# A hand-written order of 1433 steps, replaced by another order of the same steps

## The chip, the cores and the metric

One core of a Trainium2 chip runs the whole program. The metric is the device time of one execution in microseconds (us); the median of three executions of the kernel before is 490.09 us. A change of about 1% (4.9 us) is what a measurement of this kernel can tell from no change.

## What is computed

A recurrent layer over 4 batches, 8 heads, 768 positions and 48 channels a head, followed by a low-rank mix over positions and a feed-forward layer on 4 x 768 rows of 384 channels, all float32:

```python
for t in range(S):
    cur = np.einsum('bhd,bhe->bhde', u[None] * kt, vt)
    y[:, :, t] = np.einsum('bhd,bhde->bhe', rt, state + cur)
    state = wt[:, :, :, None] * state + np.einsum('bhd,bhe->bhde', kt, vt)
...
h = xt @ U @ V
u = x + h.transpose(0, 2, 1)
ch = np.maximum(u @ w_ch1, 0.0) @ w_ch2
return (u + ch).astype(np.float32)
```

## The kernel before

The recurrence is cut into 24 chunks of 128 positions, six to a batch. A chunk loads its decays w (`LW`), its r and k by channel (`LRK`), its v (`LV`) and, from the second batch on, r and k by position (`LKR`). VectorE (DVE) makes two scans of the decays (`F`, line 367, and `Q`, line 380) and scales r and k by them (`RP`, line 387, and `KS`, line 392; each may run on GpSimd instead). TensorE (PE) turns k (`KT`, line 482) and multiplies the scores (`AM`, line 495). The scores are merged with a diagonal (`SEL`, lines 430 and 432) by a predicated copy on DVE (`CP`, line 498); then PE multiplies them with v (`YA`, lines 555 and 565), adds the carried state's part (`YZ`, lines 578 and 582) and makes the state's growth (`DS`, line 505), which DVE adds up (`ZA`, line 526). The result is copied out (`XE`) and turned (`XT`, line 616). In the first batch the diagonal comes by a product (`PR`, line 448) and eight PE instructions of two columns (`MD`, line 454); later it comes by DVE or GpSimd (`RK`, `RU`, `RED`, lines 413 to 420).

When six chunks of a batch are done, the mix over positions follows (`GA`, `SELM`, `GSL`, then `HP`, line 690) and makes two blocks u of 384 positions (`UADD`, `UH`, `UL`). A block's feed-forward layer has 12 up steps (`UP`, line 738) and 12 down steps (`DN`, line 774). Each is nine matmuls of 384 columns, because each product is taken as high times high, high times low and low times high. After an up step, ScalarE (ACT) or DVE makes the rectified high part (`HH`, lines 745 and 747) and DVE the low part (`HL`, line 751); a down step needs both parts of three up steps.

The weights come as 26 pieces (12 of w1, 12 of w2, 2 of V, with U a smaller one) in a 64-bit form. Each piece takes a load (`LRAW`, line 249), two ACT instructions (`AB`, `E`), three on DVE (`C1`, `C2`, `C3`, lines 283, 290 and 297), one on GpSimd (`ADD`, line 304), a rounding (`HI`) and a subtraction (`SUB`, line 321). Up step f of a block needs piece f of w1.

Each of these is a step of its own, 1433 in all. Each engine's instructions stand in the order in which the steps are recorded, and each engine runs its own in that order. A string, `ORDER` (line 51), gives it: three digits a step, the first two the step's number, the third says in its lowest bit whether the step runs on its second engine, and in the rest how many filling matmuls stand ahead of it. `plan` (line 127) reads it; nothing else sets the order. A filling matmul (`warm` and `lead`, lines 178 and 182) multiplies constants into the bank that the step is about to overwrite; its only effect is that PE works. Loads are all issued by SyncE (SP), one after another; a load whose buffer isn't free yet holds up all loads behind it. The buffers that matter here are two for w, four for r and k (`LRK`), two for v, seven for raw weight pieces (shared with u), and three PSUM banks for the feed-forward layer.

```python
i, how = DIGITS.index(ORDER[n]) * 64 + DIGITS.index(ORDER[n + 1]), DIGITS.index(ORDER[n + 2])
if how % 2:
    s.eng = s.alt
s.lead = how // 2
```

Of the kernel before, what the change touches and what calls it, by code (L numbers as in the profile page):

```python
# [48 lines left out]

DIGITS = "0123456789ABCDEFGHIJKLMNOPQRSTUVWXYZabcdefghijklmnopqrstuvwxyz+-"  # L50
ORDER = (
    "3n03p01g01F04C00001X03s03r04E03y03u03o03v04D01h01i04e01j01G01k01H05301I01l04L04d04F00200103t13q01Z01J04H01m0"
# [4 lines left out]
    "05x05e06105J05X05f18Y05b05Y05M05g15005K06005h15Z05OA5105i01518O05a05P05w00Q05j05z00B05k00S08p05Q00C00T05R05+"
    "05m08X05l00D08o05S06300E00h00U01b06E06408y05-"
    "06515p01c05N08x06705y08Z18Q05n01d06615q00F00q01e06809F05r00V00i05s80j06901f15t01600W00k05o00H08q00l00s06A00J"
    "00m06B00K09h08a16C60L06D08b00n06F01809O00M00o02W06G08c06H60Y00N10p16I00O10r06J08d01706KE9P06O06S06L02Y06T09Q"  # L60
    "06M06P00a06N16Q01900t06U06R16V16WI1A00u06X01B00v06Y01C00w01D01y01E10x02x00X10Z00y12X06Zm0b02Z00c02a01+00d01z"
    "02b06a12z00e06b02c00f02E00g12d01p01-02y06cc2e12002+02106f02-"
    "02F06d12202G06e01r02H02N06i03002302I06g08z12J06l08+16j12406h02P06k03106o01q08-"
    "06m09R02K09q03206n02509016r0AG01s03312o02L01t08R06p06u06s02O01u09116t01v06q06x02708T02M13D01w08U06v02606y06w"
    "09E02q08V02802Q02903F02R02A06z02B09N02S02f02C01x12D12p06++8r03E02r07108s13G06-"
    "02s02h03H07002T08t07407212U01O03I02V17507303J02g02i03K03402t07602j08u01Q07702k09g08v08W13603L18g07802l01P079"
    "08e09p08h02u03e0A702m03M02v01R08k82n18f02w13507A01S08l03709S11T03808w13f08m03907B03g03h08n09H08i03O03i09J09T"
    "09208j19G03A09409301U03V07C03B09503C01V01W09903N03P07D09M13W03X03Q09I09K07M09A03R0A607N07Q09L19B0AZ09607E07O"
    "09C07R09i03S09W09707S07F09D07T17G0AF09X07P17U09809b07V03Y07W09c09j09U09d03Z09k1D409V09l07X17Y09m09e07Z09Y03a"
    "0AY09f07b07a09n1A809Z03b07e07c09a0Ah03c17d03d17f09o13T19wCA909y09x03j09+0AB03U07g08609-"  # L70
    "03k0AA03l07H0AE1A019r1Ab0AM07h09s1AN0Ag1Ac19t03m0AQ07i1Ai07I09u07j0AH1AC07k08S0AD0D30Ad0AI07J07l07m09v0AJ07n"
    "09z0DD0AK0DC0Aj1AL1AO0Ae07o0A10AP0DT0Af1A20Aa07p0DE0Ao0DU0AR07K0AS1DF07q07L0Dc0Ak1D608707r0Al0DG0Am1Dd07s07t"
    "0E30DW0A30A40DB17u07w0A50DX0D707v0An0D80Db0Ap0Av07x0De0AT07y0D90AU0D50880AV0Dw0E41Dv0DY0DA1AW07z0Df0AX0DH0Dg"
    "0Aq0E51EV07+1DI0E20Ar07-"
    "0DV0Dy0DJ0Dh1EM0800E60As0Dz0E11Ex0DK0DL0EW1810DZ0At0Eo0DN0820Di0Au0EL0D+0DM0830Da1DO1EX1D-"
    "0Aw0840DP0Ax0850En0E00Ay0EU0Dx0EO0890Az0A+0E70EP1EY0ET0Ew0A-"
    "0EQ08C08A0FN0B008B0E80B10ER08D0Eq0FD0C10B308E0FO1Er1B40B20Es0C208F0FP0FM0Ev1B70FG08I0B80B518J0Ey1B61ES0C50B9"
    "1Dj0Et08K0Dk0C31Hk0BA18L0FI0Ez0C608G0Eu1E+08H0C90Hu0BB08M0C40CA0Ht08N0Hn0BE0BC0FJ0Ho1E90BH0BF1Hv0DQ0I80Hp0EA"
    "0BD0BG0Hw0BK0BI1C71BJ0C80IH0DR0BL1BN0CB1DS0BM0CC1FH0BQ0BO1BP0BT0BR1BS0BW0BU1BV0BZ0BX0BY0Bc0Ba1Bb0Bf0Bd1Be0Bi"
    "0Bg0Bh0Bl0Bj0Bk0Bm0Bn0Bo0Br0Bp0Bq0Bs0Bt0Dn0Dl0Do0Dp0ED0Dm0Eb0Bu0Ec0Bx0Bv0Bw0By0Dq0Dr0EZ0EN0EB0Ds0EE0FE0Ea0EF"  # L80
    "0Dt0EC0Bz0Du0FQ0II0B+0FK0FL0Ef0B-0EG0Hq0C00EH0Ep0IJ1F10Ia0EI0Eg0E-"
    "0Hl0CD0F20IK0F01Eh0EJ0IB0CG0EK0Ij0Hx0ID0IC0CJ0Ik0CE1CH0CF0Hr1CI0F50CK0Hs0Ed0CL0IE0H+0Cn0H-"
    "0Ee0Il0J00Id0CM0Im1CP0Ie0If0CN1J90CO0Ei0CQ0CR0Ej0FR1FF0F30F60I90Ek0CS0F71F40FS1F80CT0IL0IG0FT0CU0Hy1Hm0JA0F9"
    "0IF0Hz1J30Co0Ib0FA0Ig0El0In0I20JS0Em0J50CV0J40Jc0JB1I30FU0JC0CY0CW0Ih0Jb0CX0FB0J60CZ0Cb0FC0Ii1Ju0Ca0Jd0FV0Cc"
    "0Cd0Je0FW0IA0Cp0FX0J10IM0K10JV0FY0IN0Ce0JX0FZ0JW0JD0K20Ch0J70Cf1J81IO0Cg0I00IP0Ci1JY0IS0JT0Fa0K31Cj0Iq0IT0Ck"
    "0Ir0I10IU1K41JG0Cl1I40JH0Ja1IQ0Cm0Io0Ic0JZ0Ip1Cq0IR0Jf0Ct0Jx0Cr0Cu0Jz0Jy0Cs0J+0Cv0Cw0Cz0Cx0Cy0C+0C-"
    "0D00Is0D10D20Iu0It0Fb0Ji0Fc0JI0Jj0I50Fd0IV0Fe0Ff0IW0JE0J20Gi0IX0Iv0Jv0Gm0Gq0JF1Gj0I60Ix0Gr0Gn0I70Fg0JJ0Iw1JU"
    "0IY0Fk0Fo0Iy0Jg1K50Fl0K00JK0Fp0IZ0Jk0JL0Iz0Jh0Fh0JN0J-0Fi0Jl0Fj0JO0K61Jw0I+0Fm1K80JM0I-"
    "0Fn1Fq0K70Jm0Gk0Fr0Fs0K90Go1Gl1Fv0Gs1Gp1Gt1Jn0Fy0Fw0Ft1Jo1Fx0Fu0F-"
    "0Fz1F+0GQ0G01G10G20G50G31G40G80G60G70GR0G91GA0GB0GE0GC0GD0GH0GF0GG0GK0GI0GJ0GN0GL0GM0GS0GO0GP0GT0GW0GU0GV0GX"  # L90
    "0GY0GZ0Gc0Ga0Gb0Gd0Ge0Gf0Gu0Gg0Gh0Gx0Gv1Gw0G+0Gy0JP0Gz0H10G-"
    "0H00JQ0H21H40JR0H30H70H50H60HA0H80H90HS0HB1HC0HT0Jp0Jq0HD0Jr0HG0HE1HF0HJ0HH0HI0HM0HK0HL0HP0HN0HO0HU0HQ1HR0Js"
    "0KA0Jt0KB0KF0KC0HV0KD0HW0HY0KE0HX0KG0HZ0KH0KI0Ha0KJ0KK0KL0KP0Hb0KM0KQ0KN1KR1KT0KO0He0Hc0KU0Hd0KS1KV0LN0KW1LR"
    "0Hf0LO0LS0LP0LT0LQ0Hg0LU1Hh0LV0KX0Hi0LW0Hj0LX1LY1Ka0KY0KZ0Kd0Kb1Kc0Kg0Ke0Kf0L50Kh0Ki0Kj0Km0Kk1Kl0Kp0Kn1Ko0L6"
    "0Kq0Kr0Ks0Kv0Kt1Ku0Ky0Kw0Kx0L70Kz0K+0K-"
    "0L20L00L10L30L40L80LB0L90LA0LC0LD0LE0LH0LF0LG0LI0LJ0LZ0LK0La1Lb0Lc0LL0LM0Lf0Ld0Le0Li0Lg0Lh0M70Lj0Lk0Ll0Lo0Lm"
    "1Ln0Lr0Lp1Lq0M80Ls0Lt0Lu0Lx0Lv1Lw0L+0Ly1Lz0M90L-"
    "0M00M10M40M21M30M51M60MA0MD0MB0MC0ME0MF0MG0MJ0MH0MI0MK0ML0MM0MN0MO0"
)


# [885 lines left out]
```

## Time and profile before

| what | us |
|---|---|
| median of 3 executions (488.08 to 491.03) | 490.09 |
| the profiled execution | 493.23 |
| its span, first to last instruction | 491.4 |
| PE busy | 467.2 |
| DVE busy | 315.2 |
| ACT busy | 169.5 |
| GpSimd (POOL) busy | 114.6 |

The profile is of one execution. PEld is the loading of weights into the array; it overlaps PE. The clock of PE is granted at one of two levels, 2.4 GHz (1.0 in the rows) and 1.2 GHz (0.5). Filling matmuls count as busy.

### The profile page before, as it was taken

To read this page: it belongs to the slowest core of one execution; us is meant where nothing else is said; L and a number is where in the kernel's file an instruction comes from. 1 tells how busy PE (TensorE), PEld (TensorE's weight loads), DVE (VectorE), ACT (ScalarE), POOL (GpSimd) and SP (SyncE) were. 2 spreads that over 40 slices of the span, in tenths; PEclk is the share of its full clock that TensorE was granted. 3 is DMA by queue.
4 is the path that set the end of the run, shared out by engine and by line. 5 is a ranking of instruction groups with operands and counts; after the bars stand their busy time and mean duration, and the time that the engine had idled before them with its cause. 6 is when DMAs were issued, how large, how long until landed. Compare 5 with 4: busy or idle time off the path is not lost.

```text
span 491.4 us, 9913 instructions
## 1 busy us (share of the span) xinstructions
PE 467.2 (95%) x4116; PEld 419.8 (85%) x4116; DVE 315.2 (64%) x543; ACT 169.5 (34%) x430; POOL 114.6 (23%) x106
## 2 busy tenths in 40 slices
...
PEclk9656999999999999999999999999999999999998
...
GB/s 295 258 70 173 232 234 128 176 130 147 148 85 88 168 269 111 108 1 16 79 166 120 192 99 33 99 21 0 17 32 1 1 34 17 1 27 23 0 18 37
DMA packets 20644, 47.38 MB, mean 96 GB/s; under 512 B 2480, under 2 KB 8880, under 8 KB 20592
## 3 DMA queue, kind: packets, MB, share of 16 engines
...
q8 instruction: 34, 0.56, 0.5%
q14 instruction: 18, 0.15, 0.1%
...
## 4 chain that ended last, share of the span: by engine, by line
PE 57%; DVE 21%; DMA 10%; ACT 4%; issue 4%; POOL 2%; SPq 0%; POOLq 0%; DVEq 0%; ACTq 0%
PE f L774 23%; PE f L738 22%; DMA raw_w<-in_w 4%; DMA w<-in_wT 3%; DVE Q L380 3%; DVE F L367 3%; DMA rk<-in_rkT 3%; PE aps L495 2%; DVE cva_w L297 2%; DVE hl L751 2%; PE y L555 1%; PE trk L482 1%; PE y L565 1%; DVE rk L392 1%; PE dS L505 1%
## 5 line engine op out<-in xcount | busy, mean ns | idle before, releaser
L738 PE MATMUL f<-u,w1h 128*128 128x384 f32 x576 | 158.1, 344 | 2.0 <-DVE hl L751 1.4
L738 PEld LDWEIGHTS f<-u,w1h 128*128 128x128 f32 x576 | 105.4, 188 | 4.8 <-DVE hl L751 2.5
L774 PE MATMUL f<-hh,w2h 128*128 128x384 f32 x288 | 100.0, 347 | 0.0
L738 PE MATMUL f<-u,w1l 128*128 128x384 f32 x288 | 97.6, 339 | 0.0
L774 PE MATMUL f<-hh,w2l 128*128 128x384 f32 x288 | 97.5, 339 | 0.0
L751 DVE SCALAR_TENSOR_TENSOR hl<-f,hh 128x384 fp32r<-128x384 f32 x96 | 52.5, 552 | 34.6 <-ACT hh L745 33.4
L745 ACT ACTIVATE hh<-f 128x384 fp32r<-128x384 f32 x56 | 27.3, 488 | 128.0 <-PE f L738 128.0
L774 PE MATMUL f<-hl,w2h 128*128 128x384 f32 x288 | 66.3, 338 | 0.0
L774 PEld LDWEIGHTS f<-hh,w2h 128*128 128x128 f32 x288 | 54.0, 188 | 3.5 <-issue 1.7
L774 PEld LDWEIGHTS f<-hh,w2l 128*128 128x128 f32 x288 | 54.1, 188 | 0.3
L738 PEld LDWEIGHTS f<-u,w1l 128*128 128x128 f32 x288 | 54.1, 188 | 0.2 <-DVE w1l L321 0.2
L774 PEld LDWEIGHTS f<-hl,w2h 128*128 128x128 f32 x288 | 52.0, 188 | 0.0
L789 DVE TENSOR_TENSOR xT<-f,xT 128x384 f32<-128x384 f32 x24 | 13.3, 553 | 55.6 <-PE f L774 55.5
L747 DVE TENSOR_SCALAR hh<-f 128x384 fp32r<-128x384 f32 x40 | 22.2, 554 | 32.2 <-PE f L738 32.0
L304 POOL TENSOR_TENSOR cva_w<-cva_w,raw_w 128x384 int32<-128x384 int32 x24 | 29.8, 1247 | 40.8 <-DVE cva_w L297 21.7
L432 POOL TENSOR_SCALAR_AFFINE_SELECT A<-dv 128x512 f32<-128x512 f32 x23 | 19.5, 855 | 84.4 <-PE y L565 46.4
L498 DVE COPY_PREDICATED A<-maskf,aps 128x1024 f32<-128x1024 uint32 x24 | 31.4, 1307 | 7.1 <-PE aps L495 4.6
L367 DVE TENSOR_TENSOR_SCAN F<-w,resets 128x517 f32<-128x517 f32 x24 | 32.5, 1354 | 2.5 <-DMA w<-in_wT 1.4
L430 ACT ACTIVATE A<-ident,dv 128x128 f32<-128x128 f32 x100 | 31.6, 390 | 5.1 <-DVE dv L461 2.3
L495 PE MATMUL aps<-rk 48*128 48x128 f32 x384 | 30.6, 303 | 2.2 <-DVE rk L392 1.3
L495 PEld LDWEIGHTS aps<-rk 48*128 48x128 f32 x384 | 25.7, 204 | 6.1 <-issue 2.6
L380 DVE TENSOR_TENSOR_SCAN Q<-w,qd 128x516 f32<-128x516 f32 x24 | 30.5, 1273 | 0.0
...
## 6 DMA issues: line engine op xcount, KB each, us to landing
...
```

The costliest lines, as they stand in the source:

```text
L304: lambda: nc.gpsimd.tensor_tensor(out=d["to"].bitcast(I32), in0=d["a"].bitcast(I32), in1=d["e"], op=ALU.add),
L367: nc.vector.tensor_tensor_scan(out=F[:, ::-1], data0=st["w"][:, ::-1], data1=resets[:, ::-1], initial=1.0, op0=ALU.mult, op1=ALU.add)
L380: nc.vector.tensor_tensor_scan(out=st["Q"], data0=st["w"][:, 0:n], data1=qd, initial=0.0, op0=ALU.mult, op1=ALU.add)
L430: nc.scalar.activation(A[:, i, j], ident, AF.Copy, scale=dv[:, NP * i + j : NP * i + j + 1])
L432: nc.gpsimd.affine_select(out=A[:, i], in_=dv[:, NP * i : NP * i + NP].unsqueeze(2).broadcast_to([P, NP, P]), pattern=[[0, NP], [1, P]], c ...
L495: nc.tensor.matmul(aps[:, i, j, :], rk[r, 1, j, :], rk[r, 0, j, :], start=True, stop=True)
L498: nc.vector.copy_predicated(flat(st["A"]), mask8, flat(st["aps"]))
L738: nc.tensor.matmul(ps, wt[:, f, ct, :], u[ct][:, z], start=(n == 0), stop=(n == 8))
L745: nc.scalar.activation(hh, d["ps", f], AF.Relu)
L747: nc.vector.tensor_scalar(out=hh, in0=d["ps", f], scalar1=0.0, scalar2=None, op0=ALU.max)
L751: nc.vector.scalar_tensor_tensor(out=hl, in0=d["ps", f], scalar=0.0, in1=hh.bitcast(F32), op0=ALU.max, op1=ALU.subtract)
L774: nc.tensor.matmul(d["o", ct], wt[:, 4 * ct + part, f - 3 * part, :], hid[f][z], start=(part == 0 and n == 0), stop=(part == 3 and n == 8),)
```

## The change

Only the string is replaced. The set of steps, their functions, buffers and dependences are the same. The diff is 47 lines of digits on either side, of which one each:

```diff
-    "3n03p01g01F04C00001X03s03r04E03y03u03o03v04D01h01i04e01j01G01k01H05301I01l04L04d04F00200103t13q01Z01J04H01m0"
+    "3n01g01F03p00004C01X03s03r04E03y03u03o03t03v01h01i04D01j01G04d01k00104e01I00201l01H05304F04L03q01Z01J04H01m0"
...
```

Read out, the new string differs in three ways: the order, the second engine for some steps (DVE has 518 steps instead of 529, ACT 300 instead of 296, GpSimd 106 instead of 99), and the filling matmuls (71 instead of 146; 31 ahead of the first `MD` in both). Before, the other 115 stand mostly ahead of the first block's up steps: 9, 24, 19 and 31 ahead of its steps 0, 1, 2 and 10. Now the other 40 stand ahead of `KT` of chunk 0 (6), `YA` of chunk 5 (22), `XT` of chunk 5 (4), `SELM` of batch 0 (4), `AM` of chunk 6 (2) and `YA` of chunk 6 (2), and none in the feed-forward layer.

The first place is SP's queue, between the loads of the first chunks. The names end in a buffer number; raw_w_3 and raw_w_0 ahead of the larger numbers are pieces 3 and 0 of w1, w the decays of a chunk. Before, pieces 3, 4 and 6 of w1 stand here:

```order
L340 DMA w_642<-in_wT 128x517
L352 DMA v_657<-in_vN 128x448
L344 DMA rk_675<-in_rkT 128x1024
L340 DMA w_698<-in_wT 128x517
L249 DMA raw_w_3_708<-in_w 128x768
L348 DMA kr_719<-in_rkN 128x768
L352 DMA v_758<-in_vN 128x448
L249 DMA raw_w_4_780<-in_w 128x768
L344 DMA rk_784<-in_rkT 128x1024
L249 DMA raw_w_6_819<-in_w 128x768
```

In the new order they stand here:

```order
L344 DMA rk_304<-in_rkT 128x1024
L249 DMA raw_w_0_362<-in_w 128x768
L249 DMA raw_w_3_373<-in_w 128x768
L340 DMA w_397<-in_wT 128x517
L352 DMA v_413<-in_vN 128x448
L340 DMA w_429<-in_wT 128x517
L249 DMA raw_w_4_502<-in_w 128x768
L249 DMA raw_w_6_526<-in_w 128x768
L340 DMA w_529<-in_wT 128x517
```

Before, w_642 and w_698 are the decays of chunks 6 and 7, and the three pieces are queued around and behind them; now w_397, w_429 and w_529 are those of chunks 4, 5 and 6, and the pieces stand ahead of them.

The second place is DVE around the predicated copy of chunk 0 (`A` written under `maskf`, L498). F and Q are scans, rk and kr the scaled and multiplied r and k, cva a weight piece in work. Before:

```order
L387 TENSOR_TENSOR rk_153<-rk_153,Q_155 128x512
L448 TENSOR_TENSOR kr_258<-rk_162 128x512
L392 TENSOR_TENSOR rk_157<-rk_157,F_176 128x512
L283 TENSOR_SCALAR cva_w_8_197<-cva_w_8_197 128x384
L461 COPY dv_272<-trd_251 128x8
L498 COPY_PREDICATED A_246<-maskf,aps_260 128x1024
L380 SCALAR_TENSOR_TENSOR Q_298<-w_139,qd 128x516
```

Now:

```order
L290 TENSOR_SCALAR cva_w_5_273<-cva_w_5_273 128x384
L297 SCALAR_TENSOR_TENSOR cva_w_8_195<-raw_w_8_143,cva_w_8_195 128x384
L297 SCALAR_TENSOR_TENSOR cva_w_5_273<-raw_w_5_189,cva_w_5_273 128x384
L367 SCALAR_TENSOR_TENSOR F_320<-w_166,resets 128x517
L448 TENSOR_TENSOR kr_323<-rk_171 128x512
L367 SCALAR_TENSOR_TENSOR F_328<-w_248,resets 128x517
L392 TENSOR_TENSOR rk_171<-rk_171,F_320 128x512
L283 TENSOR_SCALAR cva_V_292<-cva_V_292 96x384
L403 RECIPROCAL qd<-F_320 128x4
L498 COPY_PREDICATED A_254<-maskf,aps_276 128x1024
L526 TENSOR_TENSOR Z_364<-dS,Z_315 128x384
```

The copy that PE waits for in chunk 0 has moved back behind the scans of chunks 2 and 3 and the work on weight pieces 8 and 5.

The third place is PE at the start of the feed-forward layer: hp is the mix, f an up step, aps, trk, y, trx and dS the products of a chunk. Before (the pair of a weight load and a filling matmul into f_0_0_0 comes nine times):

```order
L690 MATMUL hp_0_0_893<-Vst,gs_884 128x384
L690 MATMUL hp_0_1_903<-Vst,gs_884 128x384
L690 MATMUL hp_0_2_905<-Vst,gs_884 128x384
L180 LDWEIGHTS resets
L180 MATMUL f_0_0_0_924<-resets 128x384
L180 LDWEIGHTS resets
L180 MATMUL f_0_0_0_924<-resets 128x384
```

Now:

```order
L690 MATMUL hp_0_2_990<-Vst,gs_958 128x384
L482 MATMUL trk_992<-ident,rk_660 128x128 x4
L180 LDWEIGHTS resets
L180 MATMUL y_1002<-resets 128x384
L180 LDWEIGHTS resets
L180 MATMUL y_1002<-resets 128x384
L555 MATMUL y_1002<-A_912,v_797 32x128 x8
L565 MATMUL y_1002<-A_912,v_797 32x128 x8
L616 MATMUL trx_0_1051<-ident,xT_0_1038 128x128 x3
L505 MATMUL dS<-v_797,kn_1044 48x48 x8
L738 MATMUL f_0_0_0_1069<-u_0_0_1032,w1h 128x384
L738 MATMUL f_0_0_0_1069<-u_0_0_1032,w1l 128x384
```

Chunk 6, the first of the second batch, now stands ahead of and within the first block's up steps, where filling matmuls stood.

## Rows read from the trace of the kernel before

**Rows 1.** The page's second part: PE's granted clock in 40 slices of the span.
```profile
PEclk9656999999999999999999999999999999999998
```
**Rows 2.** Busy time by stretches: sum and count of PE, PEld, DVE, ACT, POOL; clock; DMA.
```profile
12.00:24.00 12.00, 8.08 (x72) 6.50 (x72) 11.97 (x14) 7.97 (x23) 6.88 (x6) 0.71 0.83 269
24.00:36.00 12.00, 11.25 (x136) 9.52 (x135) 7.72 (x13) 8.39 (x27) 2.36 (x2) 0.50 0.19 62
36.00:48.00 12.00, 11.37 (x139) 9.68 (x131) 7.75 (x11) 7.48 (x22) 4.51 (x4) 0.66 0.52 166
48.00:60.00 12.00, 10.85 (x194) 7.86 (x191) 10.23 (x19) 8.14 (x24) 5.15 (x4) 1.00 0.77 225
...
84.00:96.00 12.00, 11.28 (x64) 10.76 (x63) 11.97 (x27) 8.08 (x22) 5.41 (x5) 1.00 0.51 181
```
**Rows 3.** The chain that ended last: start, us, what; in a stretch at full clock.
```profile
240.54 0.57 PE y L555 x16
242.21 1.09 PE aps L495 x16
...
249.12 0.59 PE trk L482 x4
249.71 1.59 PE f L738 x9
```
**Rows 4.** PE's instructions in order of time: start, us, what, idle before it.
```profile
13.97 1.05 PE L454 MATMUL trd<-u_diag,kr 128*128 128x2 f32 x8 [2.27 <-POOL kr L448]
...
38.02 2.08 PE L495 MATMUL aps<-rk 48*128 48x128 f32 x16
...
72.35 0.48 PE L738 MATMUL f<-u,w1h 128*128 128x384 f32 x1
...
74.90 4.08 PE L180 MATMUL f<-resets 128*128 128x384 bf16 x24
...
97.35 5.21 PE L180 MATMUL f<-resets 128*128 128x384 bf16 x31
102.26 0.47 PE L738 MATMUL f<-u,w1h 128*128 128x384 f32 x1
...
110.49 0.34 PE L774 MATMUL f<-hh,w2h 128*128 128x384 f32 x1
...
201.89 0.41 PE L738 MATMUL f<-u,w1h 128*128 128x384 f32 x1
...
483.46 0.34 PE L774 MATMUL f<-hh,w2h 128*128 128x384 f32 x1
```
**Rows 5.** DVE's instructions in order of time.
```profile
12.82 1.30 DVE L297 SCALAR_TENSOR_TENSOR cva_U<-raw_U,cva_U 128x192 uint32<-128x192 uint32 x1
14.05 1.75 DVE L387 TENSOR_TENSOR rk<-rk,Q 128x512 f32<-128x512 f32 x1
...
21.70 0.68 DVE L387 TENSOR_TENSOR rk<-rk,Q 128x512 f32<-128x512 f32 x1
22.30 1.23 DVE L367 TENSOR_TENSOR_SCAN F<-w,resets 128x517 f32<-128x517 f32 x1
...
24.29 0.55 DVE L297 SCALAR_TENSOR_TENSOR cva_w<-raw_w,cva_w 128x384 uint32<-128x384 uint32 x1
...
29.66 1.28 DVE L498 COPY_PREDICATED A<-maskf,aps 128x1024 f32<-128x1024 uint32 x1
...
36.43 0.56 DVE L526 TENSOR_TENSOR Z<-dS,Z 128x384 f32<-128x384 f32 x1 [2.67 <-PE y L582]
...
40.65 1.29 DVE L498 COPY_PREDICATED A<-maskf,aps 128x1024 f32<-128x1024 uint32 x1 [2.52 <-PE aps L495]
```
**Rows 6.** SP's issues in order of time, around the third weight load.
```profile
53.85 0.33 SPq L340 DMA_DIRECT2D w<-in_wT  x1
54.23 1.48 SPq L249 DMA_DIRECT2D raw_w<-in_w  x1
```
**Rows 7.** POOL's instructions in order of time.
```profile
15.22 1.62 POOL L392 TENSOR_TENSOR rk<-rk,F 128x512 f32<-128x512 f32 x1
```

More of the change, by code (lines that the diff above doesn't have):

```diff
@@ L57 @@
[L57 to L98, printed above, removed]
+    "3n01g01F03p00004C01X03s03r04E03y03u03o03t03v01h01i04D01j01G04d01k00104e01I00201l01H05304F04L03q01Z01J04H01m0"
+    "1K01n00z04G00301o10401Y01L03z11M00700503++3w01a04m04I01N15201b03-"
+    "13x04014M042C4100+00604404304J00P00901000804K10-"
@@ new lines @@
+    "04605U01105B04R01c01204714g00R04n14S04h15504N04l15610A04i04V01d04504O04P14s01300G04W01e04j04X10h04804Q11f15T"
+    "04k04T05700I05C14f04905804t00i04A00B01405u00k04B00C00j04o00l05c05W04w04p04q15D00m05X01515d16105Y05914U04r15b"
+    "04u00Q05E05A00n05H04v00D00o00q04Y05I05Z00E01600S08O05i05a05400T00s05x04Z05j05e00U01805v05y14x05F04a05z08X00F"
+    "05J05f14y10V04b05L00r05+00Y04z04c05G14+06218Y08o05V00p10W06304-08P05K06001705g18y01905k05-"
+    "00a01A00t05O05h11B00u00X15P06405w08x00v05005l08p01C05Q05100w06511y05R05M05p05N02x05S08Z15m06618R06E08Q00H05q"
@@ new lines @@
+    "05n08z00x06708T01D09F05r00J08a11+05s08U05t02z05o09E08V00K06801E00Z00L069i8b09N00M09O06A08q08c02N06B00N18d19h"
+    "00b06C80O10c08r06D02y06F00d06G08s02+08+16H82-02P08W16I03008g46J09P08-"
+    "06K08t03108h09019q06O06S08e09Q02E03206T08k4A709116P00e06L09R06M02W08u08l0AG06Q08f06N19g06U08m06R12G08i08v08n"
+    "06V16W00f09G08j10y10g18w12F02O03312Y02H02Q01z02I06Z06X02R02J09p01-"
+    "02S09S12006c06Y02K06a19T12T06b01p06f06d02L12o02102U06e02M06i06g02206h02X01r06l02Z02303D02V16j02412q02a01q06k"
+    "09402p02b02r06o01s09502c03F02d02501t09902s01u06p11v09A06m16r06q09B01O06n01w02e12701x13E09C02t06s06u03G09D06t"
@@ new lines @@
+    "02u02601Q03H06x02f02806v03I02v02906w03J06+06y02A03K03402w17102h06z02B01P06-"
+    "13L12C03e01R09202g02D1720AZ02i07403501S02j09301T03602k09607301U03g07007509i09702l01V03M01W02m03V07602n13f037"
+    "03h07M03807703i03903N07N03O03A07O07A07803X03P03B07907P13Q07B03j03R09H07Q07U07C07R03C09I19817V09J03S07D03W03k"
+    "03T03U07G03l07E07F03m07H07S19M17W07T19U07X17Y03Y09V09K03Z09Y0A607Z09j07b03a09k17a09o09l09Z07e07c19a19L17d09w"
+    "0AF03b09W07f09m09x07h09X0AY09n19+07g07i09y03c17j03d17k0A90Ah0AH17n0AA0AB0AE07l17m0AI08607o07p0Ab07I09r1Ac1Ag"
@@ new lines @@
+    "17J0AC08S0AD0D307q0Ad09s07K07L0Ae0AM07r0870AN07s0DT0DC0Af07t09t0AJ0Ai09u0DD0D607w07u0Dc0DW09b07x07v09v0DX17y"
+    "09c0Aj0A809z08809d0D40AK09-"
+    "0DE0AL1D809e0Ak0AO0A01D90A109f0AP0Dv0DA17z0Aa0Al0DF1Am1Dd0A20DB17+1AQ0A30DU0DG0Ao0E20AR0E307-"
+    "0An1A40AS0AT0DY0De0A50Ap0AU0DH0D50Av0Db0AV0Dw0DJ0Aq0DI0DK0E40Ar0DV0Df1DN0As0EM0Dy0AW0800AX0DO0Dz1E51Dg0E10At"
+    "0810DL0E60EV0Au0820Ex0Dh0Aw0DM0Eo0Di0Dj0Ax0830DZ0Dk0D70Da0EL0Ay0841EW0E90D+0Az0850890EA0Ey0A+0EX0C108C08A0EU"
+    "0Ez0C208B0EY0EO0FN0A-0B308D0B40ET0B00B70B108E0D-"
```

26 lines of the change are left out of this document (22 added, 4 removed).

## The prediction, made before the changed kernel ran

> **What bounds the kernel now.** I read the busy time by stretches first, then PE's instructions in order of time with their idle times, then DVE's. A core with one long matmul queue is bounded by PE, and PE's busy share says nothing here, because filling matmuls count as busy. So I keep a ledger. PE's work ahead of a step is the sum of all real steps ahead of it at their full-clock durations, without fills: 1.59 for each up or down step, 1.09 for the scores, 0.59 for the turning of k, 0.57 and about 0.45 for the two halves of the product with v [rows 3], and for the other steps 0.2 to 1.0, taken in the same way from start to start behind 44 us. The start of a step less this work is the time that PE has lost so far.
>
> Before, the first real step starts at 13.97 with nothing done: 14.0 lost. The first up step starts at 72.35 with 32.9 of work ahead: 39.5 lost. The fourth down step of the first block starts at 110.49 with 56.8 ahead (six MD, five KT, six AM, six YA, twelve up and three down steps and the small ones): 53.7. The first up step of the second batch starts at 201.89 with 141.2 ahead: 60.7. The last down step starts at 483.46 with 420.0 ahead: 63.4 [rows 4]. Behind 202 us PE loses 2.7 in 280 us. All that can be won lies between 14 and 202 us.
>
> What causes that loss changes. From about 17 to 44 us (0.71 over 12 to 24, 0.50, then 0.66 over 36 to 48) the clock is at its lower level, 0.5, and small steps take twice their time (scores 2.08 against 1.09) [rows 1 to 4]; there PE is the engine the others wait for: DVE is busy 7.72 and 7.75 us of 12 and has single waits of 2.67 and 2.52 us on PE [rows 2, 5]. From 48 us on DVE is busy 10.23 to 11.97 of 12 and sets the pace [rows 2]; PE then waits, and the table fills the waits: 24 and 31 fills take 4.08 and 5.21 us [rows 4], 0.158 each from start to start. The up steps start at once behind them, so these rows don't tell whether the fills outlast the waits.
>
> For DVE I keep the same ledger: the durations of its instructions ahead of a step in the table's order, at undisturbed rows (1.23 a scan, 1.28 a predicated copy, 0.68 a scaling, 0.55 the third step of a weight piece, and small ones) [rows 5]. Ahead of the first up step stand 91 DVE instructions, 56.0 us; it started at 72.35, so DVE's lag, time less work, was 16.4. At the fourth down step it was 110.49 - 93.4 = 17.1; at 201.89, with 179.9 of work, 22.0.
>
> **The change, part by part.**
>
> *The fills.* 75 of 146 go. At 0.158 that is 11.9 us of PE time. By itself it is worth between nothing (the fills stood in waits for DVE, and without other work PE waits as long) and 11.9. I take nothing, as DVE is busy almost without a stop there [rows 2], and count the real work that takes their place. That is chunks 6 and 7.
>
> *The real work moved in.* Ahead of the first up step PE now has 36.5 of work instead of 32.9 (one AM, KT, YA, XT and DS more, 3.6). Ahead of the fourth down step it has 65.0 instead of 56.8.
>
> *What DVE must have done.* Ahead of the first up step stand 118 instructions, 72.0 us, instead of 91 and 56.0: two more of either scan (4.9), four more second and third steps of weight pieces (3.6), two scalings, a predicated copy, two reductions, and small ones. At the fourth down step it is 103.3 instead of 93.4. So the feed-forward layer starts later and then runs without stopping. Over the whole kernel DVE's work falls by 4.7 us, as 11 of its steps go to ACT and GpSimd, which have idle time beside it (ACT 8.08 of 12 busy, POOL 5.41) [rows 2].
>
> *DVE's lag, the number that decides.* Ahead of the predicated copy of chunk 2 DVE has 32.7 of work instead of 26.5, that is 6.2 us of weight pieces and scans of later chunks. Before, it sat idle for 8.5 us between 24 and 48 us (24 less 7.72 and 7.75) [rows 2]. The weights for this are there: pieces 3, 4 and 6 of w1 were queued behind the decays of chunk 7, issued at 53.85 [rows 6], and are now queued ahead of the decays of chunks 4 to 6. So I take 5.4 off the lag. Bounds: nothing (the waits only move), and 8.5 (all of the idle time). The middle is near the 6.2 that the order can put there, less a wait for r and k of chunk 5, which are now queued behind the decays of chunk 6.
>
> *The sum.* First up step: 72.0 + 11.0 = 83.0, 10.7 us later than before; PE has lost 83.0 - 36.5 = 46.5, seven more than before at that step. Between there and the fourth down step DVE has 31.3 of work and PE 28.5, so both are nearly full; I let the lag grow by 1.7 instead of the 0.7 of before, to 12.7. The step then starts at 103.3 + 12.7 = 116.0, with 116.0 - 65.0 = 51.0 lost: 2.7 less than before. From there to 202 us PE lost 7.0 before: ten fills (1.6), waits for DVE, and the changes between kinds of steps. The new table has no fills there, and DVE's own limit has room: ahead of the first up step of the second batch it has 177.7, with a lag of 17 that is 194.7, while PE with 144.0 of work comes there at about 199. I take 4.0. At the end PE loses 2.7, as before. Total 51.0 + 4.0 + 2.7 = 57.7 instead of 63.4: 5.7 us won. The profiled execution would go from 493.23 to 487.5; it lies 3.1 above the median, so the median goes from 490.09 to 484.4.
>
> *Fills against the clock.* PE had waits of up to 2.27 us and the clock fell at 17 us [rows 2, 4]; from 48 us to the end, with shorter waits and the fills, it stayed at 1.0 [rows 1, 2]. The Trainium skill's page "TensorE: Matmul & The Clock Gate", section "HAM oscillation — how this bites in real kernels", says that waits between bursts of matmuls put the array back on its lower clock, and so speaks against taking fills out. The trace agrees for 17 us. By that rule the stretch before the first up step, where PE has 7.7 of work and 12 fills in 15 us, could lose the clock; by the rows it keeps it, because 22 fills stand right ahead. I keep it in the sum, and make the fall a rival.
>
> *More on GpSimd.* A scaling on DVE took 1.75 us instead of 0.68 while GpSimd ran one of 1.62 [rows 5, 7]. The skill's page "SBUF — State Buffer", section "SBUF: two separate sides", says that the two share a port pair which one of them holds for a whole instruction; the row agrees. GpSimd has seven steps more: by that rule DVE could lose up to seven times 1.1, 7.7 us, and nothing would be won; by the rows it is less, since most of its steps run beside DVE instructions of undisturbed length.
>
> **The rivals.**
>
> *The lag stays.* DVE waits for the cold PE at other places: the scores of chunks 2 and 4 still stand right ahead of the copies that need them. For it: these waits were on PE [rows 5]. Against it: there is now other DVE work between. Lag 17.6 at the fourth down step: 103.3 + 17.6 - 65.0 = 55.9, plus 6.7 is 62.6: 489.3, no change.
>
> *The array stays cold (the slower side).* The first chunks now go at DVE's pace, so PE may never be dense enough before 48 us to get its clock back. Up to the second half of chunk 1 (13.9 of work, about 43 us) the forecast has it cold anyway. From there to the product with v of chunk 5 there are 14.9 of work; at half clock 29.8, so 72.8, and 22 fills at 0.32 bring it to 79.8, where the forecast has 68. The chain from there to the first up step takes some 13.5 (93), DVE's 31.3 and the growth of 1.7 give 126 for the fourth down step: 61.0 lost, and with 6.7 more 67.7: 494.4. It decides if the clock comes back later than about 60 us. For it: 27 us at 0.5 before. Against it: PE has more to do than it can at half clock, so it will be dense.
>
> *The clock falls between 68 and 83 us.* The first two up steps then take 3.2 each; 3.2 us: 487.6.
>
> *All of the idle time is used.* Lag 9.5 at the fourth down step: 47.8 lost, and 3.0 and 2.7 behind it: 53.5, so 480.2.
>
> **How the numbers follow.** Forecast 0.46, within 481 to 488; the lag stays 0.18; cold 0.15; the clock falls 0.08; all used 0.13. About 1% (4.9 us) is what a measurement can tell from no change. Faster by over 1% (below 485.2): the last case and some seven tenths of the forecast, 0.46. Slower by over 1% (above 495.0): most of the cold case, as its price is a lower one if the fills don't bring the clock back, 0.12. The rest, 0.42, lies within. The range leaves out part of the cold case above and of the last one below: 479.5 to 494.5.
>
> **What would show it.** Right: the first up step near 83 us, ten us later than before; DVE busy over 10 of 12 us from 24 us on; the clock back by 50; no stop of PE over 1 us in the first block; the second batch's first up step near 199. The forecast is wrong if the fourth down step starts behind 119 us, or if PE's loss between there and 200 us is 7 or more.

## The result, and the profile of the changed kernel

The changed kernel takes 482.94 us (median of 4 executions, 482.59 to 484.70); the kernel before, measured again beside it, takes 490.56. The ratio is 0.9862, with a 95% interval of 0.9823 to 0.9902: faster, by 1.0 to 1.8%. The forecast was 484.4. The profiled execution took 483.14 with a span of 481.4, against 493.23 and 491.4 before; so the two traces differ by 10.0 us where the medians differ by 7.6, and the traces' differences are to be read with that in mind.

First the page's busy times and PE's clock, to be held beside [rows 1], then the busy times by stretches, with the columns of [rows 2]:

```profile
PE 449.4 (93%) x4041; PEld 409.8 (85%) x4041; DVE 314.6 (65%) x532; ACT 171.2 (36%) x446; POOL 119.9 (25%) x113
...
PEclk9786999999999999999999999999999999999999
```

```profile
24.00:36.00 12.00, 8.18 (x105) 6.88 (x105) 12.00 (x19) 10.60 (x34) 2.12 (x2) 0.83 0.58 191
36.00:48.00 12.00, 10.11 (x108) 8.44 (x110) 9.75 (x15) 6.45 (x19) 6.07 (x6) 0.60 0.33 96
48.00:60.00 12.00, 9.40 (x217) 7.74 (x215) 11.26 (x20) 12.00 (x39) 5.40 (x5) 1.00 0.87 295
...
72.00:84.00 12.00, 8.54 (x97) 6.45 (x96) 11.91 (x23) 9.12 (x26) 3.79 (x4) 1.00 0.71 250
```

PE's busy time fell by 17.8 us (467.2 to 449.4) while the traced time fell by 10. The real matmuls are the same in both, so what went is fills and time at the lower clock. From 24 to 48 us DVE is busy 21.75 us instead of 15.47. The clock is not one stretch at 0.5 as before, but comes and goes until 45.6 us, and is full from there to 479.

PE's instructions in order of time, with the up and down steps of [rows 4]: the fills and the turning of k of chunk 0, the first up step, the fourth down step, the first up step of the second batch, the last down step:

```profile
18.22 2.08 PE L180 MATMUL trk<-resets 128*128 128x384 bf16 x6 [4.07 <-DVE dv L461]
20.09 1.06 PE L482 MATMUL trk<-ident,rk 128*128 128x128 f32 x4
...
81.77 0.44 PE L738 MATMUL f<-u,w1h 128*128 128x384 f32 x1
...
112.96 0.33 PE L774 MATMUL f<-hh,w2h 128*128 128x384 f32 x1
...
194.50 0.42 PE L738 MATMUL f<-u,w1h 128*128 128x384 f32 x1
...
473.55 0.34 PE L774 MATMUL f<-hh,w2h 128*128 128x384 f32 x1
```

With the real work ahead of each step (36.5, 65.0, 144.0 and 420.0 us in the new order) PE's ledger reads as follows. "Lost" is the start of a step less this work.

| step | lost, before | forecast | lost, after |
|---|---|---|---|
| first up step | 39.5 | 46.5 | 45.3 |
| fourth down step | 53.7 | 51.0 | 48.0 |
| first up step of the second batch | 60.7 | 55.0 | 50.5 |
| last down step | 63.4 | 57.7 | 53.5 |

DVE's lag (start less DVE's work ahead) at the first up step is 81.77 - 72.0 = 9.8, at the fourth down step 112.96 - 103.3 = 9.7; before it was 16.4 and 17.1. The busy times from 12 us to the first up step, before and now, show where the lag went: DVE sat idle for 12.4 us then and for 4.9 now.

```profile
12.00:72.35 60.35, 51.31 (x623) 38.62 (x623) 47.99 (x74) 40.35 (x112) 24.98 (x22) 0.77 0.62 199
```

```profile
12.00:81.77 69.77, 52.18 (x706) 38.80 (x703) 64.84 (x102) 49.15 (x141) 26.94 (x26) 0.85 0.62 206
```

What PE waited for longest, from the view of waits (us in total, times, longest); all three are DVE:

```profile
PE trk L180 <- DVE dv L461: 4.1, 1, 4.1
PE y L555 <- DVE A L498: 3.4, 5, 1.3
PE aps L495 <- DVE A L498: 2.9, 2, 1.9
```

DVE had waits of 2.67 and 2.52 us on PE in [rows 5]. Between 24 and 48 us one is left, ahead of the predicated copy of chunk 2 (the second row; the first is the copy of chunk 1):

```profile
38.16 1.27 DVE L498 COPY_PREDICATED A<-maskf,aps 128x1024 f32<-128x1024 uint32 x1
41.67 1.32 DVE L498 COPY_PREDICATED A<-maskf,aps 128x1024 f32<-128x1024 uint32 x1 [2.25 <-PE aps L495]
```

### The profile page after: what moved, and what is told of

Read it like the earlier page. It is cut to its first block, busy times and chain, and to the rows that moved or that the text cites. A ratio compares the mean times of both kernels' runs of the same rounds, so it can differ in the third digit from the quotient of the medians.

```text
span 481.4 us, 9783 instructions
## 1 busy us (share of the span) xinstructions
PE 449.4 (93%) x4041; PEld 409.8 (85%) x4041; DVE 314.6 (65%) x532; ACT 171.2 (36%) x446; POOL 119.9 (25%) x113
## 4 chain that ended last, share of the span: by engine, by line
PE 70%; DVE 16%; DMA 5%; ACT 4%; issue 3%; POOL 1%; SPq 0%; ACTq 0%; DVEq 0%; POOLq 0%
PE f L774 29%; PE f L738 28%; PE aps L495 3%; DVE F L367 3%; DVE A L498 2%; DMA v<-in_vN 2%; PE y L555 2%; DVE cva_w L297 1%; DMA raw_w<-in_w 1%; PE trk L482 1%; DVE Q L380 1%; PE y L565 1%; PE trx L616 1%; DMA rk<-in_rkT 1%; DVE cva_w L283 1%
## 5 line engine op out<-in xcount | busy, mean ns | idle before, releaser
L738 PE MATMUL f<-u,w1h 128*128 128x384 f32 x576 | 157.0, 343 | 1.6 <-DVE u L705 0.8
L738 PEld LDWEIGHTS f<-u,w1h 128*128 128x128 f32 x576 | 105.3, 188 | 4.5 <-DVE u L705 1.5
L738 PE MATMUL f<-u,w1l 128*128 128x384 f32 x288 | 97.5, 338 | 0.0
L745 ACT ACTIVATE hh<-f 128x384 fp32r<-128x384 f32 x52 | 25.2, 486 | 137.6 <-PE f L738 137.5
L738 PEld LDWEIGHTS f<-u,w1l 128*128 128x128 f32 x288 | 54.1, 188 | 0.0
L747 DVE TENSOR_SCALAR hh<-f 128x384 fp32r<-128x384 f32 x44 | 24.2, 552 | 31.0 <-PE f L738 30.7
L430 ACT ACTIVATE A<-ident,dv 128x128 f32<-128x128 f32 x112 | 35.6, 392 | 24.8 <-PE y L565 16.1
L498 DVE COPY_PREDICATED A<-maskf,aps 128x1024 f32<-128x1024 uint32 x24 | 31.5, 1313 | 11.4 <-PE aps L495 5.7
L304 POOL TENSOR_TENSOR cva_w<-cva_w,raw_w 128x384 int32<-128x384 int32 x24 | 28.3, 1182 | 42.1 <-DVE cva_w L297 16.7
L432 POOL TENSOR_SCALAR_AFFINE_SELECT A<-dv 128x512 f32<-128x512 f32 x20 | 15.9, 804 | 75.5 <-PE y L565 58.9
L380 DVE TENSOR_TENSOR_SCAN Q<-w,qd 128x516 f32<-128x516 f32 x24 | 32.5, 1354 | 0.1
```

The costliest lines, as they stand in the source:

```text
L304: lambda: nc.gpsimd.tensor_tensor(out=d["to"].bitcast(I32), in0=d["a"].bitcast(I32), in1=d["e"], op=ALU.add),
L380: nc.vector.tensor_tensor_scan(out=st["Q"], data0=st["w"][:, 0:n], data1=qd, initial=0.0, op0=ALU.mult, op1=ALU.add)
L430: nc.scalar.activation(A[:, i, j], ident, AF.Copy, scale=dv[:, NP * i + j : NP * i + j + 1])
L432: nc.gpsimd.affine_select(out=A[:, i], in_=dv[:, NP * i : NP * i + NP].unsqueeze(2).broadcast_to([P, NP, P]), pattern=[[0, NP], [1, P]], c ...
L498: nc.vector.copy_predicated(flat(st["A"]), mask8, flat(st["aps"]))
L738: nc.tensor.matmul(ps, wt[:, f, ct, :], u[ct][:, z], start=(n == 0), stop=(n == 8))
```

## The experiments

Twelve kernels ran; all change the string only. Ratios are to the kernel before. In four of them (without fills, and with the old engines throughout) the string has eight lines fewer, so their rows name lines that are eight lower: L738 is L730 there.

### The fills

Before, the order as it was, without 115 of its 146 fills (the third digit of a step holds them; one step of eleven is shown):

```diff
-6Zm   (UP 0.0.1 of batch 0, 24 fills)
+6Z0
```

> The order before, without the 115 fills behind the first 31; nothing else. Mine (VectorE sets the pace behind 48 us, the fills stand in waits for it): 490 +- 3, the waits of TensorE grow by what the fills took. Rival A, the fills outlast the waits: up to 18 us faster (115 x 0.158), 472 to 485. Rival B, the fills hold the clock: the clock goes back to 0.5 somewhere between 60 and 110 us and the time is 494 or more.

Measured: 495.41 us, ratio 1.0103 (1.0056 to 1.0150): slower, and rival B's case. The busy times by stretches:

```profile
72.00:84.00 12.00, 8.55 (x25) 7.14 (x24) 9.84 (x24) 6.41 (x13) 5.07 (x5) 0.50 0.41 131
...
96.00:108.00 12.00, 7.06 (x30) 6.75 (x29) 10.59 (x21) 6.95 (x17) 2.36 (x3) 0.72 0.47 151
```

PE's waits between 70 and 113 us in the same run, and its first up step and fourth down step:

```profile
PE f L730 <- DVE w1l L313: 7.3, 2, 4.9
```

```profile
70.08 0.69 PE L730 MATMUL f<-u,w1h 128*128 128x384 f32 x1 [2.45 <-ACT u L691]
...
112.11 0.34 PE L766 MATMUL f<-hh,w2h 128*128 128x384 f32 x1
```

The first up step comes 2.3 us earlier (70.08), as no fills stand ahead of it: here the fills did outlast the wait. But PE now waits 7.3 us for two weight pieces, with no fills in these waits, and the clock falls to 0.5 for the whole of 72 to 84 us and again in 96 to 108. By the tenth up step (95.44, before 95.65) the lead is used up; in the eleventh PE waits 4.9 us for its piece and then runs at 0.5. The fourth down step comes at 112.11: 55.3 lost, 1.6 more than before. So the fills did hold the clock, and taking them out costs more than it saves: 1.6 us there by the traces, 4.0 by the medians (the kernel before took 491.44 beside this run).

The new order without its other 40 fills, and without only the six ahead of the turning of k of chunk 0:

```diff
-69i   (YA 5, 22 fills, and five more steps: 40 fills)
+690
-42C   (KT 0, 6 fills: the second kernel, this step alone)
+420
```

> The new order, without the 40 fills behind the first 31; nothing else. Mine: 483 +- 3 as VectorE sets the pace. Rival B, the fills hold the clock: it falls to 0.5 in 60 to 85 us, or does not come back at 22 us, and the time is 486 to 494. Rival A: up to 6 us faster (40 x 0.158), 477 to 480.

> The new order without the 6 fills ahead of the turning of k of chunk 0 alone. Rival D, these 6 fills bring the clock back at 21.7 us and that is worth something: the clock stays at 0.5 from 15 to 44 us as before, 485 to 490. Mine: the clock there may well stay low, but TensorE waits for VectorE there, so 483 +- 2.

Without the 40: 485.69 us, ratio 0.9890 (0.9847 to 0.9934). The interval overlaps that of the changed kernel, so the 2.8 us between the medians are not sure by themselves. The time lies in my own range; the clock does what rival B said, and the trace has a like sum there. The busy times and the first up step:

```profile
72.00:84.00 12.00, 9.91 (x67) 5.95 (x67) 10.88 (x21) 7.47 (x20) 4.20 (x4) 0.50 0.66 236
```

```profile
84.62 0.69 PE L730 MATMUL f<-u,w1h 128*128 128x384 f32 x1
```

The clock is 0.5 over 72 to 84 us where it is 1.00 with the fills, and the first up step comes at 84.62 instead of 81.77, 2.9 later. What the lower clock by itself costs is not shown by this, for two reasons. The profiled execution is the slowest of its four (487.23, mean granted clock 0.940); the fastest took 483.65 at 0.966. And the fills don't hold the clock all the way: this kernel's fell at 68.8 us, while in all eight traces that keep the 22 fills and the order of the changed kernel up to the first up step it is 1.00 over 60 to 76 us; but in seven of these eight it then goes to 0.5 for 3.4 to 10.2 us between 76 and 89. The changed kernel's own trace is the one exception, and its other three executions have lower mean clocks (0.971, 0.964 and 0.963 against 0.976). The longest such fall is in the kernel below that relieves GpSimd:

```profile
72.00:84.00 12.00, 7.89 (x82) 6.30 (x79) 10.33 (x20) 9.05 (x25) 1.98 (x2) 0.67 0.61 212
```

There the clock is 0.5 from 76.0 to 86.3 us, and the fourth down step comes at 112.69, no later than the changed kernel's 112.96.

Without the six: 484.40 us, ratio 0.9872 (0.9831 to 0.9913), no difference that can be told. The clock still comes back, at 23.4 us, but for 3.4 us only; over 24 to 36 us it is 0.62 instead of 0.83, and chunk 1's scores start at 30.96 instead of 30.65:

```profile
24.00:36.00 12.00, 8.78 (x86) 7.13 (x86) 12.00 (x19) 8.78 (x27) 2.42 (x2) 0.62 0.48 169
```

DVE is busy 12.00 of 12 in either, so a faster PE gains little there. A clock that stays at 0.5 throughout, rival D's case, did not come about.

### Order and engines apart

The new order with each step on its old engine, and the old order with each step on its new one (138 steps differ; two are shown):

```diff
 new order, old engines
-8z0   (RK 7 on GpSimd)
+8z1   (RK 7 on VectorE)
 old order, new engines
-9o1   (KS 9 on VectorE)
+9o0   (KS 9 on GpSimd)
```

> The new order and its fills, but each step on the engine that it had before (11 steps go back to VectorE). Mine: the order makes the gain, so 483 to 485, since the 4.7 us of VectorE's work lie mostly behind 100 us. Rival C, the relief of VectorE makes the gain: 487 to 490.

> The order and the fills of before, but each step on the engine that the new table gives it (138 steps change, VectorE has 11 fewer). If the choice of engines is worth something of its own: 484 to 488. If it is worth something only with the order for which it was chosen: 488 to 494, no change or slower.

| | old engines | new engines |
|---|---|---|
| old order | 1 | 1.0065 (1.0025 to 1.0105) |
| new order | 0.9979 (0.9945 to 1.0013) | 0.9862 (0.9823 to 0.9902) |

The new order alone takes 489.62 us, the new engines alone 493.90. My expectation for the first, 483 to 485, is refuted: neither part brings the gain by itself. The trace of the new order with the old engines shows where it goes. PE in order of time: the turning of k of chunk 0, the first up step, the fourth down step, the first up step of the second batch, a wait for the state, an up step behind it, the last down step:

```profile
16.23 1.06 PE L474 MATMUL trk<-ident,rk 128*128 128x128 f32 x4
...
82.67 0.44 PE L730 MATMUL f<-u,w1h 128*128 128x384 f32 x1
...
114.45 0.34 PE L766 MATMUL f<-hh,w2h 128*128 128x384 f32 x1
...
198.97 0.42 PE L730 MATMUL f<-u,w1h 128*128 128x384 f32 x1
...
204.91 0.56 PE L497 MATMUL dS<-v,kn 128*48 128x48 f32 x16 [1.44 <-DVE Z L518]
...
207.53 0.52 PE L730 MATMUL f<-u,w1l 128*128 128x384 f32 x1
...
480.69 0.34 PE L766 MATMUL f<-hh,w2h 128*128 128x384 f32 x1
```

Lost: 46.2, 49.5, 55.0 and, at the last down step, 60.7. At the fourth down step 4.3 of the gain of 5.7 are there, with the old engines. Behind it PE loses 5.5 to the second batch, where the changed kernel loses 2.5, and 5.7 more to the end, where it loses 3.0. Held step by step against the changed kernel's trace, this is spread over eight places, each 0.5 to 1.3 us worse, most of them waits for DVE (a part is made good between them); behind the one of 1.44 the clock falls, as the 0.52 of a matmul at 207.53 shows (0.34 elsewhere). Over 194 to 320 us, the new order with the old engines and the changed kernel:

```profile
194.00:320.00 126.00, 122.63 (x1276) 113.82 (x1275) 88.77 (x143) 38.43 (x101) 29.99 (x27) 0.99 0.29 89
```

```profile
194.00:320.00 126.00, 124.27 (x1299) 114.57 (x1295) 84.11 (x134) 43.12 (x116) 30.42 (x28) 1.00 0.29 89
```

DVE is busy 4.7 us more with the old engines, ACT as much less.

In the old order with the new engines the clock is back by 36 us, and the first up step comes 5.7 us earlier than before, at 66.70; all of that is given back: 2.8 by the fourth down step, 2.2 more by the second batch, and 1.4 behind it. By stretches, and PE in order of time:

```profile
36.00:48.00 12.00, 10.68 (x203) 8.58 (x203) 11.79 (x19) 9.49 (x27) 5.61 (x4) 1.00 0.69 218
```

```profile
66.70 0.48 PE L738 MATMUL f<-u,w1h 128*128 128x384 f32 x1
...
107.64 0.34 PE L774 MATMUL f<-hh,w2h 128*128 128x384 f32 x1
```

PE's waits there, between 66 and 108 us:

```profile
PE f L738 <- DVE hl L751: 3.0, 2, 1.9
```

From the first up step to the fourth down step DVE has 36.9 us of work for PE's 23.9, and is busy for 37.9 of the 40.9 us that pass. The loss is 33.8, 50.8, 60.1 and 64.2. So half of the early start is lost to DVE's work on the weights, which still lies ahead; where the rest goes was not traced.

Two more kernels take the old engines only behind the first up step of the second batch, and only ahead of it; a third takes only the 57 changed steps of the feed-forward layer's high parts back to their old engines:

```diff
 late: behind UP 0 of block 0 of batch 1
-Fi1   (UH 2.0.0 on VectorE)
+Fi0   (UH 2.0.0 on ScalarE)
 early: ahead of it
-8z0   (RK 7 on GpSimd)
+8z1   (RK 7 on VectorE)
 HH and UH alone
-6d0   (HH 0.0.2 on ScalarE)
+6d1   (HH 0.0.2 on VectorE)
```

> The new order and fills; the new choice of engines up to the first up step of the second batch, that of before behind it. In the run with the old engines throughout, TensorE lost 4.5 us more than in the new kernel up to that step and 3.4 more in the next 117 us. If these two losses are separate: 485.5 to 487.5, with TensorE's loss at that step at 50 to 51.5. If the late choice does not matter: 482 to 484.

> The new order and fills; the choice of engines of before up to the first up step of the second batch, the new one behind it. If the losses are separate: 486.5 to 488.5, with a loss of 54 to 55.5 at that step and 1.5 to 2.5 in the next 117 us. If the early loss is made good later: 483 to 485.

> The new kernel, with the rectified parts (HH) and the high parts of u (UH) alone on the engines of before; 57 steps change between ScalarE and VectorE, the count on either hardly. If the loss of the run with all old engines comes from which step of the feed-forward layer runs where: 486 to 490. If it comes from the steps of the recurrence and of the weights: 482 to 485.

Late: 486.64 us, ratio 0.9897 (0.9849 to 0.9945); PE loses 4.5 us in the 117 us behind the step (52.2, a little above the 50 to 51.5 expected, to 56.8), against 1.7 in the changed kernel. Early: 487.63, ratio 0.9925 (0.9889 to 0.9961); 53.5 lost at the step instead of 50.5, and 1.5 behind it. So the two losses are separate, as far as can be told: by the traces 3.8 and 2.8 us at the end, 6.6 together, where the old engines throughout cost 7.1; by the medians 3.7 and 4.7, 8.4 together, against 6.7 (the early run's profiled execution is the fastest of its ten). The step's loss in the early run was a little below the 54 to 55.5 expected. The high parts alone: 484.06, ratio 0.9903 (0.9877 to 0.9929), 1.1 above the changed kernel, with overlapping intervals. By subtraction most of the cost then belongs to the other 81 steps, those of the recurrence, the weights and the low parts of u. Those were not run alone.

### The work ahead of the copy of chunk 2

Two kernels put VectorE steps that the new order has ahead of the predicated copy of chunk 2 back behind it: twelve (5.7 us), then nine (weight pieces alone, about 4 us); the texts written ahead of the runs count eleven and eight. With them go, as they share the pieces' buffers or results, a load, four steps on ACT and two or three on GpSimd.

```diff
 twelve steps, in the new order behind CP 2 (4v0)
+1b0 1c0 1f1 0B0 0k0 0C0 0l0 5W0 0m0 5X0 151 5Y0   (C2, C3, SUB of piece 8 of w1, ...)
 nine steps: 5W0 5X0 5Y0 (F, T, R of chunk 4) stay ahead
```

> The new order, but eleven VectorE steps (pieces 8 and 3 of w1 and the first of V, two scans' parts of chunk 4, one subtraction; 5.7 us) stand behind the predicated copy of chunk 2 instead of ahead of it; what needs them follows. Mine (the lag is won because this work lies in VectorE's waits): the lag at the first up step grows from 9.8 to between 12.5 and 15, and the time to 485.5 to 488. Rival, the waits only move and the lag is won elsewhere: lag 9 to 11, 482 to 484.

> As the run with eleven VectorE steps put behind the predicated copy of chunk 2, but only the eight steps of the weight pieces (18, 3 of w1 and the first of V; 3.9 us); the scan of chunk 4 and its parts stay, so that the GpSimd scaling of chunk 4 that held TensorE for 10 us there is not late. Mine: the copy of chunk 2 comes at about 41 to 42 us as in the new kernel, and the 3.9 us are paid behind it: the lag at the first up step is 12 to 14, the time 485 to 487.5. Rival, it was only the late scan that cost time: 482 to 484.

Twelve: 494.63 us, ratio 1.0084 (1.0055 to 1.0113), outside both expectations. The copy of chunk 2 starts at 41.88 instead of 41.67, though 5.7 us less work stands ahead of it. That doesn't show that the work cost the copy nothing: in this run PE's clock is 0.5 from 16.5 to 43.8 us, and the copy waits 3.23 us for PE's scores. Then PE stands still for 10 us. PE, ACT and GpSimd of this run, in order of time:

```profile
54.16 1.08 PE L482 MATMUL trk<-ident,rk 128*128 128x128 f32 x4 [10.06 <-POOL cva_V L304]
```

```profile
53.05 0.52 ACT L314 ACTIVATE w1h<-cva_w 128x384 fp32r<-128x384 f32 x1 [2.38 <-POOL cva_w L304]
53.48 0.58 ACT L486 ACTIVATE kn<-trk 128x512 f32<-128x512 f32 x1
```

```profile
49.33 1.80 POOL L392 TENSOR_TENSOR rk<-rk,F 128x512 f32<-128x512 f32 x1 [4.23 <-DVE F L367]
51.09 1.93 POOL L304 TENSOR_TENSOR cva_w<-cva_w,raw_w 128x384 int32<-128x384 int32 x1
```

The row of PE names an addition of V that ends at about the right time and has nothing to give to `trk`. Read backwards by what each step needs: the bank of `trk` is emptied by ACT's copy of the k of chunk 3 (`kn`, to 54.06); this copy stands on ACT behind the rounding of a weight piece; the rounding waits for GpSimd's addition (to 53.02); the addition stands on GpSimd behind the scaling of chunk 4's k; and this scaling waits 4.23 us for the late scan.

Nine: 492.43 us, ratio 1.0024 (0.9984 to 1.0064), a lag of 17.5 at the first up step: all of the gain is gone, against an expected 485 to 487.5. Here the copy does come earlier, at 38.47, by 3.2 us, so the pieces were not free ahead of it. The price is paid behind it, in the same queue of ACT without the late scan. PE (the turning of k of chunk 3, then of chunk 4, and the scores of chunk 4), DVE and ACT of this run, in order of time:

```profile
38.29 1.12 PE L482 MATMUL trk<-ident,rk 128*128 128x128 f32 x4
...
47.58 1.11 PE L482 MATMUL trk<-ident,rk 128*128 128x128 f32 x4 [6.31 <-ACT kn L486]
...
59.59 1.16 PE L495 MATMUL aps<-rk 48*128 48x128 f32 x16
```

```profile
38.47 1.31 DVE L498 COPY_PREDICATED A<-maskf,aps 128x1024 f32<-128x1024 uint32 x1 [2.25 <-PE aps L495]
```

```profile
41.73 0.52 ACT L314 ACTIVATE w1h<-cva_w 128x384 fp32r<-128x384 f32 x1 [4.50 <-POOL cva_w L304]
...
45.65 0.55 ACT L261 ACTIVATE cva_w<-raw_w 128x384 f32<-128x384 f32 x1 [1.78 <-DVE w1l L321]
46.52 0.52 ACT L314 ACTIVATE w1h<-cva_w 128x384 fp32r<-128x384 f32 x1 [0.32 <-POOL cva_w L304]
46.95 0.58 ACT L486 ACTIVATE kn<-trk 128x512 f32<-128x512 f32 x1
```

The k of chunk 3 was turned by 39.4 us, but the copy that empties its bank (`kn`) stands on ACT behind the roundings of the weight pieces, which wait for GpSimd's additions, which wait for DVE. So PE waits 6.3 us for a copy of 0.58, and its clock falls: it is 0.5 from 44.8 to 58.5 us. The scores of chunk 4 start at 59.59 instead of 53.45, 6.1 later (the changed kernel's row is below), and the lag never comes back. How much of the 6.1 is the wait and how much the clock was not parted.

```profile
53.45 1.16 PE L495 MATMUL aps<-rk 48*128 48x128 f32 x16 [0.97 <-DVE A L498]
```

### GpSimd's share in the first 84 us

Eight subtractions of weight pieces moved from VectorE to GpSimd, and six steps moved from GpSimd to VectorE:

```diff
 eight to GpSimd
-0O1   (SUB of piece 0 of w1, on VectorE)
+0O0
 six to VectorE
-4M0   (PR 1 on GpSimd)
+4M1
```

> The new kernel with eight subtractions of the weight pieces in the first 84 us on GpSimd instead of VectorE, which has 4.4 us less to do there. If only VectorE's own work counts: 2 to 4 us faster, 479 to 481. If GpSimd's instructions lengthen VectorE's by about as much (in the trace of the new kernel VectorE's instructions that overlap GpSimd's seven subtractions are 4.4 us longer than undisturbed ones, 0.63 each): no change, 481.5 to 484.

> The new kernel with six steps of the first 84 us taken from GpSimd to VectorE (a product of chunk 1, two subtractions, three for the diagonals of chunks 7 and 8; 3.5 us more for VectorE). If only VectorE's own work counts: 1.5 to 3.5 us slower, 484.5 to 486.5. If undisturbed VectorE instructions give it back: 482 to 484.

484.64 us, ratio 0.9904 (0.9867 to 0.9941), and 484.00, ratio 0.9879 (0.9834 to 0.9923): neither can be told from the changed kernel. Busy times over 12 to 84 us, the changed kernel, then eight to GpSimd, then six to VectorE:

```profile
12.00:84.00 72.00, 54.41 (x718) 41.03 (x716) 67.07 (x107) 51.38 (x148) 26.94 (x26) 0.86 0.63 212
```

```profile
12.00:84.00 72.00, 55.76 (x708) 41.94 (x707) 66.97 (x99) 50.55 (x144) 37.68 (x33) 0.81 0.61 204
```

```profile
12.00:84.00 72.00, 57.24 (x710) 43.35 (x709) 66.90 (x113) 51.71 (x148) 21.75 (x20) 0.78 0.64 212
```

DVE is busy 67.07, 66.97 and 66.90 us, whether it has 107, 99 or 113 instructions there, and the first up step comes at 81.77, 83.18 and 82.09. Counted up to that step instead of to a fixed time, DVE is busy 64.84, 66.15 and 64.99 us. A pair of instructions of the changed kernel shows how that comes about; the step of a weight piece (L283), 0.35 by itself, takes 1.07 beside GpSimd's subtraction:

```profile
61.83 1.07 DVE L283 TENSOR_SCALAR cva_w<-cva_w 128x384 f32<-128x384 f32 x1
```

```profile
61.69 1.00 POOL L321 TENSOR_TENSOR w1l<-cva_w,w1h 128x384 fp32r<-128x384 f32 x1 [2.34 <-ACT w1h L314]
```

The Trainium skill's page "Perfetto Trace Analysis", section "Optimizing Scalar/DVE Operations", says that moving work between these two engines may not help, as they share a port. The two runs agree: 4.4 us less on DVE and 3.5 us more left its busy time where it was, within 0.2 us over the stretch and 1.3 up to the first up step.

No version that ran beats the changed kernel.

## Why the prediction was right, and where it was not

**The size.** The forecast gain was 5.7 us; the medians show 7.6 and the traces 10.0. That the median came so near, 482.94 for 484.4, is in part luck: the forecast carried over the 3.1 us by which the profiled execution before lay above its median, but that of the changed kernel lies within 0.2 of its own. So the profiled execution, forecast at 487.5, took 483.14, and the ledger's last loss, forecast at 57.7, is 53.5.

**The stretch and the direction.** Right: the gain is made between 14 and 202 us. Lost at the first up step of the second batch fell by 10.2 us (60.7 to 50.5), the span by 10.0. "Ten us later than before" for the first up step, and then without stopping, is what the trace shows: 81.77, and in the 31 us to the fourth down step PE lost 2.7 (14.2 in 38 us before).

**DVE's lag.** Right in kind, under-sized. The prediction took 5.4 off the lag of 16.4; 6.6 went. It let the lag grow by 1.7 to the fourth down step; it stayed where it was (9.8 and 9.7). These two terms are 3.0 us. The order does put DVE to work where it sat idle (21.75 us busy over 24 to 48, instead of 15.47; up to the first up step 7.4 us less idle). But the picture behind it, that work in idle time is free and late work costs its own length, was too simple. Put behind the copy again, the pieces cost 9.5 us (492.43 against 482.94; by the two ratios 8), not the 4 that they last: they hold up ACT's queue, and a copy that PE waits for stands behind them. So these runs show that the lag hangs on where this work stands; what the filled idle time is worth without that wait and the fall of the clock behind it, they don't show.

**The loss behind the fourth down step.** The prediction had 4.0 to the second batch and 2.7 behind it; measured are 2.5 and 3.0. This is the term whose cause the prediction missed. It named DVE's 4.7 us less, as a result of the new engines, and gave them no term of their own. With the new order and the old engines these terms are 5.5 and 5.7, and the time is 489.62: no gain that can be told. The steps as predicted hold only with the new engines, and those alone make the old order slower. So the time was right, but the gain is not the order's alone, as the sum had it; it comes from both together.

**The fills.** Taking nothing for them, out of nothing to 11.9, held for the whole change, but not for the reason given. Without other work in their place, taking out the old order's fills costs about 4 us by the medians, since they held the clock. The rule weighed in the prediction (the Trainium skill, "TensorE: Matmul & The Clock Gate", "HAM oscillation — how this bites in real kernels") speaks for them, and both runs without fills agree: 0.5 over 72 to 84 us. In the changed kernel's trace the clock kept full between 68 and 83 us, as forecast. Up to 76 us that is the fills; behind it, luck: seven of the eight traces with these fills have a fall by 84 us. So the chance of 0.08 was too low. The price of 3.2 stays open: the run without fills lost 2.9 at the first up step, and the run with the longest fall lost nothing by the fourth down step.

**More on GpSimd.** Up to 7.7 us by the rule, less by the rows: right. Summed over all DVE instructions that overlap one of GpSimd's, each less the median of its kind without, DVE's lengthening is 24 to 25 us before and about 28 after: 3 to 4 more. One reading behind it was off: DVE's scaling of 14.05 to 15.80 us ran mostly beside GpSimd's product of 13.88 to 15.25, which began first, and not beside the scaling of 1.62, which began at 15.22.

**The signs named.** First up step near 83: 81.8. DVE busy over 10 of 12 us from 24 us: 12.00, 9.75 and 11.26, so one stretch missed. The clock back by 50: at 45.6. No stop of PE over 1 us in the first block: one of 1.28, ahead of `YA` of chunk 7. The second batch near 199: 194.5.

**The rivals.** The lag that stays and the cold array fell. "All of the idle time is used" (480.2, loss 53.5 at the end) is what the profiled execution shows to the tenth, 53.5, though with other terms (47.8, 3.0 and 2.7 there; 48.0, 2.5 and 3.0 measured); the median, 482.94, lies between it and the forecast.

What stays open: which of the other 81 steps' engines carry the rest of the 6.7 us, why they cost the old order time, and what a fall of the clock near the first up step costs. The waits are many and small, and no single one was taken away.
